# Another order of the loads and of GpSimd's operations in an RWKV-7 recurrence with a wave mixer

## The chip, the cores and the metric

The kernel runs on one core of a Trainium2 chip. The metric is device microseconds of one execution. Times of several executions are given as a median with the lowest and highest; the profile is of one more execution, whose span (first to last instruction) is a little shorter than its time.

## The reference

Two stages, one after the other. The first is a recurrence over 768 tokens for 4 x 8 heads with 40 features:

```python
for t in range(S):
    y[:, :, t] = np.einsum('bhd,bhde->bhe', rt, state)
    Sa = np.einsum('bhde,bhe->bhd', state, at)
    state_decay = state * wt[:, :, None, :] - np.einsum('bhd,bhe->bhde', Sa, bt)
    state = state_decay + np.einsum('bhd,bhe->bhde', vt, kt)
```

The second takes y as x, of 4 x 768 x 320, and mixes tokens and channels:

```python
theta = x @ w_theta
zr, zi = x * np.cos(theta), x * np.sin(theta)
u = x + einsum('ts,bsd->btd', w_tok_r, zr) + einsum('ts,bsd->btd', w_tok_i, zi)
out = u + np.maximum(u @ w_ch, 0.0)
```

## The kernel before, in words

The tokens are cut into 24 chunks of 128, six for each of the four batches. A chunk's six inputs (w, k, b, a, v, r) are loaded from HBM in the arrangement of the recurrence, so w, k, b and a come as 1024 pieces of 160 bytes (`load`, line 409); r, and v of the first eight chunks, come two chunks at a time in longer pieces (`loads`, line 421). For a chunk ScalarE takes the logarithm of w (L445), TensorE sums it over the tokens, ScalarE takes exponentials (L469, L479, L487). GpSimd scales k, b and a with them (`product`, L429; the tiles kb and ah) and casts v and r (`cast`, L435). TensorE transposes these (L391, L538), makes four score matrices (L569), which VectorE or ScalarE masks on the way out of PSUM (L578, L580; where ScalarE does it, GpSimd clears the other triangle, L582), and forms the state and the output x (L610 to L684, L793 to L802). VectorE adds the state's old value to the new (the tile sum, L663) and GpSimd scales it (gt, L667).

The mixer follows in pieces. Pairs of chunks of x are transposed (L711) and multiplied by w_theta (L763, L773). Once a batch has its six chunks, or half of them, ScalarE computes sine and cosine (cs, L850, with a change of its function table before and after, the table loads at L850 and L1024), GpSimd multiplies by x (zr and zi, L865), and TensorE mixes the tokens (L881, twelve matmuls of a 128-token block with zr and zi of all six chunks). The token weights come in 12 loads of 128 rows that GpSimd's queue issues (`wtok_block`, L960, tiles wrow_r and wrow_i), which convert to bf16 on the way; TensorE transposes them (L968). The two other weights are loaded by GpSimd's queue as well (`mixer_weights`, L932).

The program is a list of some 1600 operations, each with its engine. They are made in the order of the algorithm and issued in the order of the written-out list `ORDER` (line 26); `PICK` says which operations run on their second engine, `HOMES` which PSUM bank each result gets. Each engine runs its instructions strictly in that order and waits for semaphores of the others. SyncE issues the 180 loads, stores and transposing DMAs in the list's order as well. Besides waiting for its buffer to be free, each DMA of SyncE waits for the one eight places before it in its queue, so up to eight are under way.

Filler matmuls (`WARM`, L1019) are put ahead of a few of TensorE's operations at the start.

Of the kernel before, what the change touches and what calls it, by code (L numbers as in the profile page):

```python
# [26 lines left out]
    0, 7, 3, 6, 1, 2, 20, 8, 21, 23, 24, 4, 27, 9, 32, 30, 5, 22, 31, 33, 12, 25, 26, 34, 11,  # L27
    28, 10, 69, 35, 36, 29, 70, 37, 18, 47, 44, 40, 19, 48, 72, 45, 38, 41, 71, 49, 73, 39, 46,
    98, 119, 76, 99, 58, 14, 42, 100, 74, 57, 15, 13, 120, 122, 101, 50, 121, 79, 75, 51, 123,
    53, 106, 102, 107, 131, 108, 80, 52, 16, 77, 109, 132, 125, 78, 43, 103, 81, 17, 110, 134,  # L30
    126, 111, 133, 82, 56, 84, 137, 54, 104, 124, 138, 112, 129, 83, 85, 87, 130, 88, 127, 55,
    156, 86, 128, 59, 157, 89, 146, 184, 143, 90, 147, 105, 158, 61, 97, 60, 139, 187, 159,
    135, 62, 144, 148, 164, 96, 188, 160, 165, 191, 140, 93, 136, 145, 161, 166, 141, 91, 185,
    167, 213, 186, 92, 194, 214, 149, 189, 142, 162, 168, 150, 215, 163, 169, 190, 216, 195,
    152, 221, 170, 234, 151, 246, 192, 222, 235, 193, 237, 217, 95, 236, 202, 238, 218, 94,
    196, 203, 197, 63, 241, 155, 247, 171, 267, 248, 219, 239, 199, 198, 172, 220, 223, 205,
    249, 200, 240, 271, 64, 244, 272, 242, 299, 245, 201, 154, 273, 224, 243, 300, 173, 301,
    261, 206, 254, 274, 302, 225, 174, 262, 303, 279, 153, 175, 258, 306, 176, 255, 212, 259,
    263, 280, 250, 177, 204, 281, 256, 211, 275, 496, 282, 260, 320, 226, 251, 305, 257, 208,
    252, 276, 264, 283, 253, 317, 207, 227, 349, 327, 265, 277, 497, 328, 304, 309, 278, 329,  # L40
    498, 284, 266, 310, 270, 499, 330, 350, 285, 307, 351, 268, 318, 286, 354, 308, 269, 331,
    352, 500, 311, 361, 332, 319, 287, 314, 353, 312, 209, 336, 333, 539, 362, 210, 337, 289,
    356, 288, 315, 363, 313, 322, 290, 364, 338, 355, 291, 387, 325, 292, 339, 316, 365, 540,
    388, 359, 366, 389, 541, 357, 360, 340, 390, 341, 382, 358, 391, 321, 116, 503, 113, 501,
    542, 412, 373, 181, 342, 334, 376, 374, 502, 392, 367, 411, 326, 504, 377, 375, 506, 335,
    393, 368, 505, 323, 178, 369, 545, 524, 394, 378, 370, 507, 517, 525, 413, 508, 372, 526,
    384, 371, 509, 395, 416, 396, 527, 532, 417, 528, 397, 510, 511, 514, 529, 544, 117, 595,
    512, 572, 533, 415, 383, 530, 118, 398, 573, 515, 596, 513, 554, 385, 399, 534, 531, 574,
    418, 597, 401, 535, 400, 516, 575, 414, 402, 543, 379, 324, 404, 114, 567, 598, 536, 403,
    546, 548, 115, 380, 581, 642, 576, 582, 555, 601, 549, 577, 381, 583, 599, 66, 386, 550,  # L50
    584, 537, 557, 568, 600, 551, 182, 522, 558, 602, 183, 585, 586, 538, 619, 578, 561, 587,
    419, 179, 518, 559, 547, 604, 519, 556, 427, 180, 428, 421, 429, 605, 560, 420, 606, 520,
    423, 552, 607, 626, 553, 562, 434, 422, 627, 564, 435, 425, 436, 565, 563, 643, 628, 424,
    437, 644, 610, 566, 629, 426, 613, 645, 603, 588, 611, 630, 231, 523, 571, 521, 589, 438,
    430, 570, 698, 635, 631, 646, 612, 439, 431, 636, 632, 440, 608, 745, 432, 614, 699, 647,
    609, 746, 700, 675, 648, 747, 637, 433, 615, 676, 616, 701, 293, 569, 633, 677, 748, 634,
    651, 649, 638, 678, 590, 652, 684, 296, 579, 685, 679, 617, 639, 228, 620, 621, 580, 653,
    706, 657, 591, 654, 680, 592, 618, 686, 650, 593, 661, 703, 687, 594, 441, 622, 711, 702,
    640, 442, 681, 712, 662, 688, 655, 658, 705, 656, 689, 659, 641, 663, 660, 682, 704, 664,
    690, 749, 667, 683, 665, 691, 68, 709, 692, 707, 67, 710, 729, 668, 65, 670, 672, 666, 708,  # L60
    694, 693, 750, 624, 695, 730, 719, 713, 697, 751, 720, 731, 696, 232, 732, 294, 233, 297,
    714, 721, 295, 733, 738, 298, 229, 734, 739, 715, 716, 230, 740, 735, 717, 754, 450, 752,
    451, 778, 755, 718, 346, 625, 452, 779, 453, 741, 343, 623, 756, 881, 780, 454, 757, 408,
    882, 781, 742, 405, 673, 671, 764, 883, 767, 765, 669, 782, 884, 444, 722, 455, 783, 443,
    768, 456, 766, 445, 784, 446, 736, 457, 885, 785, 458, 760, 737, 743, 447, 459, 753, 448,
    786, 787, 887, 744, 761, 796, 788, 769, 758, 460, 759, 789, 763, 461, 888, 762, 790, 462,
    797, 912, 463, 792, 791, 913, 793, 723, 770, 795, 892, 771, 914, 794, 674, 893, 915, 886,
    772, 802, 890, 464, 891, 803, 773, 347, 465, 916, 348, 344, 799, 917, 905, 805, 409, 345,
    406, 726, 920, 407, 804, 896, 811, 466, 921, 473, 897, 725, 410, 474, 808, 475, 918, 724,
    467, 809, 468, 898, 922, 469, 899, 798, 927, 476, 449, 471, 477, 919, 906, 900, 801, 889,  # L70
    928, 470, 478, 929, 960, 728, 807, 480, 901, 930, 481, 961, 955, 923, 482, 806, 962, 483,
    963, 894, 935, 727, 484, 931, 479, 924, 800, 969, 895, 485, 908, 970, 940, 486, 983, 932,
    964, 941, 902, 965, 1030, 971, 907, 934, 903, 925, 972, 1031, 776, 819, 933, 820, 1032,
    926, 487, 904, 810, 821, 1033, 488, 822, 775, 984, 936, 966, 985, 774, 938, 986, 823, 1035,
    937, 824, 939, 777, 489, 1086, 973, 825, 490, 987, 1007, 491, 1034, 949, 494, 946, 942,
    812, 492, 813, 950, 1087, 957, 1037, 814, 1088, 974, 1036, 943, 1089, 951, 815, 975, 956,
    945, 816, 990, 944, 817, 947, 958, 1041, 1039, 989, 1042, 976, 909, 818, 1040, 988, 948,
    1014, 911, 977, 826, 1015, 991, 952, 910, 1052, 827, 953, 1016, 1090, 967, 1058, 994, 1017,
    992, 968, 959, 1053, 954, 995, 979, 993, 978, 1008, 1018, 1133, 1054, 996, 1019, 980, 998,
    997, 1001, 981, 1020, 1009, 999, 828, 982, 1023, 1002, 1092, 1134, 1010, 829, 1024, 1000,  # L80
    830, 1091, 1135, 1004, 1110, 1049, 1005, 1136, 835, 1093, 1011, 836, 833, 1095, 831, 1003,
    1063, 1012, 1050, 1096, 837, 838, 1064, 1097, 1006, 1038, 1021, 1065, 1098, 1022, 1051,
    1013, 1025, 1066, 1104, 1045, 1026, 1043, 1072, 1061, 1044, 839, 1105, 840, 1060, 1073,
    1067, 1027, 1046, 1059, 1068, 1266, 1074, 841, 1047, 1069, 1267, 1161, 1075, 1048, 1028,
    1094, 1268, 1117, 1111, 1138, 1099, 1029, 1118, 1076, 1055, 1101, 1269, 1100, 1139, 1119,
    1137, 1056, 1077, 1112, 1120, 1140, 1070, 1126, 1071, 1142, 1102, 1057, 1106, 1127, 1062,
    1144, 1143, 1121, 1113, 1128, 1312, 1103, 1122, 1107, 1145, 1078, 865, 1123, 1108, 1115,
    866, 1129, 867, 1313, 1141, 1166, 1290, 1148, 1314, 1124, 1114, 1130, 1155, 1167, 1315,
    1152, 1125, 1156, 1270, 1146, 1291, 1168, 1273, 1149, 1169, 868, 1153, 1157, 1147, 869,
    1272, 1150, 1131, 1116, 1151, 1271, 1079, 1154, 1132, 1162, 870, 1080, 1170, 1109, 871,  # L90
    1277, 1316, 1292, 1275, 1171, 1278, 1340, 1158, 1367, 1276, 1317, 1172, 1159, 1297, 1173,
    1081, 1318, 1163, 1368, 1082, 1298, 1083, 1274, 1164, 1369, 1281, 1174, 1284, 1319, 1342,
    1084, 1370, 1299, 1085, 1321, 1282, 1293, 1300, 1320, 842, 1327, 843, 844, 1322, 1283,
    1165, 1301, 1305, 845, 1302, 846, 1185, 1285, 1323, 1345, 1341, 1306, 847, 1187, 1160,
    1324, 1343, 1307, 1346, 1286, 1184, 1331, 848, 1347, 1175, 1332, 1295, 1348, 1186, 858,
    1349, 859, 1344, 1373, 1176, 1333, 860, 1308, 861, 1325, 1191, 1407, 1354, 862, 1326, 1355,
    863, 1372, 1350, 1309, 1408, 1371, 1310, 864, 1409, 1351, 849, 1467, 1311, 1334, 1356, 850,
    1190, 1410, 1294, 1279, 1335, 1177, 1280, 1412, 1391, 1178, 1328, 1296, 1392, 1374, 1357,
    851, 1336, 1330, 852, 1329, 853, 1375, 1411, 1393, 1352, 854, 1358, 1394, 1287, 1414, 856,
    1353, 1303, 1400, 1288, 1304, 1179, 1413, 1401, 1395, 1468, 1180, 1469, 1188, 1396, 1289,  # L100
# [956 lines left out]
```

## Time and profile before

| | |
|---|---|
| median of 3 runs | 198.48 us (198.17 to 200.91) |
| the profiled execution | 199.53 us, its span 197.8 us |
| granted TensorE clock | 1.0 over the whole span |
| busy: PE, DVE, ACT, POOL | 187.6, 164.3, 151.7, 145.1 us |
| DMA | 32.75 MB in 134644 packets, 124816 of them under 512 bytes |
| queue of SyncE's loads (q1), queue of GpSimd's (q0) | 75.1% and 9.6% of 16 engines' span |

An engine's idle time before an instruction stands in brackets in the timelines, with what ended it. PE is TensorE; its matmuls are pipelined, and their ends are modelled. SPq, ACTq and POOLq are the sequencers that issue DMAs.

### The profile page before, as it was taken

To read this page: it belongs to the slowest core of one execution; us is meant where nothing else is said; L and a number is where in the kernel's file an instruction comes from. 1 tells how busy PE (TensorE), PEld (TensorE's weight loads), DVE (VectorE), ACT (ScalarE), POOL (GpSimd) and SP (SyncE) were. 2 spreads that over 40 slices of the span, in tenths; PEclk is the share of its full clock that TensorE was granted. 3 is DMA by queue.
4 is the path that set the end of the run, shared out by engine and by line. 5 is a ranking of instruction groups with operands and counts; after the bars stand their busy time and mean duration, and the time that the engine had idled before them with its cause. 6 is when DMAs were issued, how large, how long until landed. Compare 5 with 4: busy or idle time off the path is not lost.

```text
span 197.8 us, 8019 instructions
## 1 busy us (share of the span) xinstructions
PE 187.6 (95%) x3288; PEld 150.3 (76%) x3288; DVE 164.3 (83%) x261; ACT 151.7 (77%) x337; POOL 145.1 (73%) x210
## 2 busy tenths in 40 slices
PE   7888999999989999999999999999999999999992
PEld 6776787777768788878878888888887878767661
DVE  5269899999989999888887988999999988675453
ACT  3584979799889988979988598888998986575111
POOL 8267544679879999699799939769699697558100
PEclk9999999999999999999999999999999999999999
DMA  6999879989999999999998899988998274863055
GB/s 119 210 212 163 154 161 196 182 166 197 233 174 173 207 171 185 190 185 223 153 210 168 153 187 170 188 148 169 182 155 163 43 177 102 87 194 104 0 191 174
DMA packets 134644, 32.75 MB, mean 166 GB/s; under 512 B 124816, under 2 KB 134608, under 8 KB 134608
## 3 DMA queue, kind: packets, MB, share of 16 engines
q1 hardware_dynamic: 131680, 29.19, 75.1%
q0 software_dynamic: 2784, 2.97, 9.6%
q8 instruction: 25, 0.41, 0.9%
q10 hardware_dynamic: 144, 0.08, 0.1%
q14 instruction: 11, 0.09, 0.1%
HBM read 29.54 MB, written 3.93 MB: 169 GB/s over the span
## 4 chain that ended last, share of the span: by engine, by line
PE 68%; DMA 9%; ACT 8%; SPq 6%; DVE 3%; issue 3%; POOL 1%; ACTq 0%; DVEq 0%; POOLq 0%
PE ps_s L881 17%; PE ps_s L391 10%; PE ps_d L569 9%; PE ps_s L763 5%; SPq L409 4%; DMA raw_w<-in_w_dram 3%; DMA raw_kb<-in_k_dram 3%; PE ps_s L711 3%; PE ps_s L652 2%; PE ps_s L629 2%; SPq L421 2%; DMA raw_r<-in_r_dram 2%; PE ps_s L538 2%; PE ps_s L773 2%; ACT cs L850 2%
## 5 line engine op out<-in xcount | busy, mean ns | idle before, releaser
L429 POOL TENSOR_TENSOR kb<-raw_kb,ex 128x320 bf16<-128x320 f32 x46 | 36.8, 811 | 9.7 <-DMA raw_kb<-in_k_dram 3.3
L881 PE MATMUL ps_s<-zr,wtok_r 128*128 128x320 bf16 x132 | 37.6, 299 | 0.0
L881 PE MATMUL ps_s<-zi,wtok_i 128*128 128x320 bf16 x132 | 37.5, 299 | 0.0
L578 DVE TENSOR_TENSOR lamu<-ps_d,mask_p 128x1024 bf16<-128x1024 f32 x22 | 26.8, 1219 | 1.7 <-PE ps_d L569 1.6
L578 DVE TENSOR_TENSOR psi<-ps_d,mask_p 128x1024 bf16<-128x1024 f32 x22 | 26.8, 1218 | 1.6 <-PE ps_d L569 1.4
L578 DVE TENSOR_TENSOR lamv<-ps_d,mask_p 128x1024 bf16<-128x1024 f32 x17 | 20.7, 1218 | 2.6 <-PE ps_d L569 1.8
L429 POOL TENSOR_TENSOR ah<-raw_a,we 128x320 bf16<-128x320 f32 x22 | 19.0, 866 | 3.6 <-DMA raw_a<-in_a_dram 1.6
L578 DVE TENSOR_TENSOR phi<-ps_d,mask_n 128x1024 bf16<-128x1024 f32 x17 | 20.7, 1218 | 0.9 <-PE ps_d L569 0.8
L865 POOL TENSOR_TENSOR zi<-cs,xp 128x320 bf16<-128x320 f32 x21 | 16.9, 816 | 3.3 <-ACT cs L850 3.3
L881 PEld LDWEIGHTS <-wtok_r 128*128 128x128 bf16 x144 | 14.0, 97 | 4.5
L569 PE MATMUL ps_d<-aT,kbT 64*128 64x128 bf16 x384 | 17.1, 217 | 0.2
L881 PEld LDWEIGHTS <-wtok_i 128*128 128x128 bf16 x144 | 14.1, 98 | 3.5
L391 PE MATMUL ps_s<-wide,kb 128*128 128x128 bf16 x184 | 15.0, 223 | 1.0 <-POOL kb L429 0.7
L865 POOL TENSOR_TENSOR zr<-cs,xp 128x320 bf16<-128x320 f32 x19 | 15.3, 810 | 0.7 <-ACT cs L850 0.7
L667 POOL TENSOR_TENSOR gt<-sum,ex 128x320 bf16<-128x320 f32 x13 | 9.5, 733 | 8.0 <-DVE sum L663 4.8
L800 PE MATMUL ps_s<-kb,lamv 128*128 128x40 bf16 x192 | 15.0, 180 | 0.0
L802 PE MATMUL ps_s<-kb,lamu 128*128 128x40 bf16 x192 | 14.9, 179 | 0.0
L569 PEld LDWEIGHTS <-kbT 64*128 64x128 bf16 x384 | 11.8, 94 | 3.1 <-ACT kbT L394 1.0
L800 PEld LDWEIGHTS <-lamv 128*128 128x128 bf16 x192 | 13.2, 96 | 0.6
L887 DVE TENSOR_TENSOR up<-ps_s,xp 128x320 bf16<-128x320 f32 x22 | 10.7, 488 | 3.5 <-PE ps_s L881 3.1
L435 POOL CAST r<-raw_r 128x640 bf16<-128x640 f32 x12 | 8.6, 720 | 6.5 <-DMA raw_r<-in_r_dram 6.5
L445 ACT ACTIVATE lw<-raw_w 128x320 bf16<-128x320 f32 x24 | 11.4, 475 | 2.6 <-DMA raw_w<-in_w_dram 2.6
(176 smaller groups left out, 606.7 us busy)
## 6 DMA issues: line engine op xcount, KB each, us to landing
raw_w<-in_w_dram SPq DMA_DIRECT2D x24, 160.0 KB, 4.1
raw_v<-in_v_dram SPq DMA_DIRECT2D x24, 160.0 KB, 3.9
raw_a<-in_a_dram SPq DMA_DIRECT2D x24, 160.0 KB, 4.2
raw_kb<-in_k_dram SPq DMA_DIRECT2D x24, 160.0 KB, 3.7
raw_kb<-in_b_dram SPq DMA_DIRECT2D x24, 160.0 KB, 4.0
raw_r<-in_r_dram SPq DMA_DIRECT2D x24, 160.0 KB, 4.4
out_dram<-oo SPq DMA_DIRECT2D x9, 160.0 KB, 2.0
wrow_i<-in_moe_w_tok_i_dram POOLq DMA_DIRECT2D x6, 192.0 KB, 5.3
```

The costliest lines, as they stand in the source:

```text
L391: nc.tensor.transpose(out=dst[:, c:c + 128], in_=pair(src, g), identity=ident)
L429: pool = ("POOL", lambda: nc.gpsimd.tensor_tensor(out=dst, in0=in0, in1=in1, op=ALU.mult))
L445: add("ACT", "ln", i, lambda: nc.scalar.activation(out=paired(lw)[:, :, :, 0:D], in_=paired(raw_w[s4]), func=AF.Ln), 473, [("raw_w", s4)], ...
L569: nc.tensor.matmul(t[:, q, g, :], lhsT=lhs[g][rows(q)], rhs=rhs[g][rows(q)], start=True, stop=True)
L578: add("DVE", kindm, i, lambda: nc.vector.tensor_tensor(out=flat, in0=whole(), in1=mask.to_broadcast([128, 2 * G, 128]), op=ALU.mult), 1217 ...
L667: add("POOL", "wgt", i, lambda: nc.gpsimd.tensor_tensor(out=new_state, in0=sum_t, in1=wm.to_broadcast([128, 8, D]), op=ALU.mult), 830, [(" ...
L763: nc.tensor.matmul(ps(pk)[:, 0:DM], lhsT=lhs[:, 3 * c + kt, :], rhs=wt[:, 3 * c + kt, :], start=kt == 0, stop=kt == 2, skip_group_check=n ...
L800: nc.tensor.matmul(o, lhsT=lamv[:, p, g, :], rhs=kb[:, 0, h, 0:D], start=first, stop=False, skip_group_check=True)
L802: nc.tensor.matmul(o, lhsT=lamu[:, p, g, :], rhs=kb[:, 1, h, 0:D], start=False, stop=True, skip_group_check=True)
L865: pool = ("POOL", lambda: nc.gpsimd.tensor_tensor(out=dst, in0=in0, in1=in1, op=ALU.mult))
L881: nc.tensor.matmul(acc(), lhsT=wtok[nm][j][:, s], rhs=zs[c][:, s], start=n == 0 and c == 0, stop=n == NT - 1 and c == 1)
L887: add("DVE", "uadd", q, lambda: nc.vector.tensor_tensor(out=u, in0=acc(), in1=x, op=ALU.add), 488, [pk, x_key(q)], [u_key(q)], at="row")
```

## The change

Only the list `ORDER` differs: the same operations in another order. PE's, DVE's and ACT's own sequences come out the same; SyncE's and GpSimd's do not. The diff replaces the whole list; its first lines and those with the later token loads (operations 181 and 178):

```diff
-    0, 7, 3, 6, 1, 2, 20, 8, 21, 23, 24, 4, 27, 9, 32, 30, 5, 22, 31, 33, 12, 25, 26, 34, 11,
+    0, 3, 7, 6, 1, 20, 2, 21, 23, 8, 24, 27, 4, 30, 32, 31, 22, 33, 5, 25, 12, 34, 11, 26, 69,
...
-    542, 412, 373, 181, 342, 334, 376, 374, 502, 392, 367, 411, 326, 504, 377, 375, 506, 335,
-    393, 368, 505, 323, 178, 369, 545, 524, 394, 378, 370, 507, 517, 525, 413, 508, 372, 526,
...
+    396, 527, 384, 181, 418, 413, 532, 528, 397, 510, 178, 511, 529, 514, 545, 417, 595, 117,
```

In words, with positions counted in each engine's own sequence from 0 (a letter with a number is a load or an operation of that chunk; z(c, j) is the product zr or zi of chunk j of a batch):

SyncE, 180 positions. Moved are:
- 1 to 11: a0 ahead of half of v0; r0's second half, w2 and a1 one earlier, k1 from 8 to 11.
- 35 to 38: b5 ahead of w6, k5 ahead of k6.
- 50 to 55: w9 and k8 one earlier, r8's first half from 50 to 52; w10 and a8 change places.
- 60 to 70: w11 behind v9, w12, k10, b10, a10 and v11 two or three earlier; k11 from 62 to 70, r10's first half from 63 to 67.
- 77 to 97: b13 from 77 to 80, k14 from 85 to 87, v14 from 89 to 86, others by one.
- 128 to 145: v20, r20, b21, v21 earlier by two to five, w22, k22, b22, b23 later by three to five, others by one to three.

GpSimd, 185 positions, of which 18 are issues of weight loads. Moved are:
- 13 and 14 (k and b of chunk 3); 20 to 22 and 24, 25: the cleared lamv of chunk 3, b5, v6's cast one earlier, a5's product two later.
- 29 to 59: the first two token loads come directly one after the other (29 and 31 become 29 and 30), k7 and b7 one earlier, a7 two later. The third and fourth token load go from 33 and 35 to 36 and 39, behind r6's cast (36 becomes 35). Batch 0's first products: one goes from 45 to 34, one from 44 to 37, one from 39 to 45, the others move by one or two; k8 and b8 come one and three later. Token load wrow_i of block 4 goes from 59 to 53, ahead of batch 0's second six products.
- 60 to 91: neighbours change places; token loads of blocks 5 and 6 one and two earlier, w_ch's second load two earlier, phi of chunk 12 two earlier and psi of chunk 12 four later.
- 92 to 107: batch 1's products in another order, with v14's cast from 102 to 95, k14 and b14 three and four earlier.
- 108 to 154: mostly neighbours; batch 2's first products move by up to eight, lamv of chunk 17 four later, of chunk 18 three earlier, b21 two earlier, b22's k two later.
- From 155 on nothing moves.

185 rows, old and new, of the table ORDER are left out of this document.

## The prediction

> **What bounds it now.** I read the page first, then busy time by stretches, then the chain of waits where TensorE is not full, then the timelines of the queues that the change reorders.
>
> ```profile
> PE 187.6 (95%) x3288; PEld 150.3 (76%) x3288; DVE 164.3 (83%) x261; ACT 151.7 (77%) x337; POOL 145.1 (73%) x210
> ...
> PE 68%; DMA 9%; ACT 8%; SPq 6%; DVE 3%; issue 3%; POOL 1%; ACTq 0%; DVEq 0%; POOLq 0%
> ```
>
> ```profile
> 0.00:40.00 40.00, 35.75 (x628) 29.27 (x629) 30.57 (x61) 28.04 (x69) 23.89 (x49) 1.00 0.90 176
> 40.00:60.00 20.00, 18.38 (x371) 14.86 (x367) 18.86 (x24) 18.26 (x44) 16.83 (x24) 1.00 1.02 190
> 60.00:160.00 100.00, 99.46 (x1871) 81.80 (x1870) 91.53 (x134) 88.71 (x195) 87.23 (x121) 1.00 0.94 171
> 160.00:198.00 38.00, 34.03 (x431) 24.39 (x428) 23.32 (x44) 16.68 (x32) 17.13 (x20) 1.00 0.50 127
> ```
>
> The columns are the stretch, its length, then PE, PEld, DVE, ACT, POOL. TensorE carries 68% of the chain and is the bound. Its idle time is length minus busy: 40.00 - 35.75 = 4.25 us before 40 us, 1.62 us from 40 to 60, 0.54 us in the hundred after that, 3.97 us in the tail. A change that leaves TensorE's list alone can win only idle time, and the tail's operations are not touched. So the gain has to come from before 60 us, and a loss can come from anywhere that a GpSimd product or a load becomes late.
>
> The loads are the trouble before 60 us: DMA share 0.90 and 1.02. One of them stands in the chain. This is the chain of waits from 44 to 60 us, then ScalarE's, VectorE's and TensorE's timelines around that place.
>
> ```profile
> 48.11 6.82 DMA raw_w<-in_w_dram
> ...
> 54.95 0.03 ACT lw L445
> ...
> 55.33 0.36 ACT nuT L394
> ```
>
> ```profile
> 52.66 1.28 ACT L1024 ACT_TABLE_LOAD   x1
> 54.95 0.47 ACT L445 ACTIVATE lw<-raw_w 128x320 bf16<-128x320 f32 x1 [1.01 <-DMA raw_w<-in_w_dram]
> ```
>
> ```profile
> 56.88 1.23 DVE L578 TENSOR_TENSOR lamu<-ps_d,mask_p 128x1024 bf16<-128x1024 f32 x1 [0.60 <-PE ps_d L569]
> ```
>
> ```profile
> 54.58 0.30 PE L679 MATMUL ps_s<-wide,gt 128*128 128x80 bf16 x4
> 55.73 0.44 PE L711 MATMUL ps_s<-wide,xp 128*128 128x128 bf16 x5 [0.85 <-ACT nuT L394]
> ```
>
> The load of w for chunk 9 is issued at 48.11 and lands 6.82 us later. ScalarE, done with its table load at 52.66 + 1.28 = 53.94, waits for it until 54.95. Behind that logarithm is queued the copy of nuT, and for the bank that this copy frees TensorE's transposes at L711 wait 0.85 us. This is the largest single stall after 10 us.
>
> **The change part by part.** The lists of PE, DVE and ACT are the same instruction for instruction; only SyncE's and GpSimd's move.
>
> ```profile
> 45.01 0.60 POOL L960 DMA_DIRECT2D wrow_i<-in_moe_w_tok_i_dram  x1
> ...
> 46.43 0.59 POOL L960 DMA_DIRECT2D wrow_r<-in_moe_w_tok_r_dram  x1
> ...
> 47.80 0.59 POOL L960 DMA_DIRECT2D wrow_i<-in_moe_w_tok_i_dram  x1
> ...
> 49.18 0.59 POOL L960 DMA_DIRECT2D wrow_r<-in_moe_w_tok_r_dram  x1
> 50.15 0.71 POOL L435 CAST r<-raw_r 128x640 bf16<-128x640 f32 x1 [0.38 <-DMA raw_r<-in_r_dram]
> ...
> 55.64 0.80 POOL L429 TENSOR_TENSOR kb<-raw_kb,ex 128x320 bf16<-128x320 f32 x1 [1.66 <-DMA raw_kb<-in_k_dram]
> ```
>
> ```profile
> 45.81 0.54 SPq L409 DMA_DIRECT2D raw_kb<-in_b_dram  x1
> 46.44 1.57 SPq L421 DMA_DIRECT2D raw_r<-in_r_dram  x1
> 48.11 0.55 SPq L409 DMA_DIRECT2D raw_w<-in_w_dram  x1
> 48.70 1.37 SPq L409 DMA_DIRECT2D raw_kb<-in_k_dram  x1
> ```
>
> ```profile
> q0 software_dynamic: 573, 0.78, 58.9%
> ```
>
> Loads at 46 to 49 us. Chunk 9's w and chunk 8's k go ahead of the half of r (46.44). So w is issued at 46.44 instead of 48.11. Even if it still takes 6.82 us it lands at 53.26, before ScalarE asks at 53.94. And it should take less: the four token-weight loads hold 58.9% of the DMA engines from 46 to 54 us (q0, last row), 0.589 x 8 / 4 = 1.18 us of all 16 engines each, and two of them are moved behind. The stall of 1.01 us goes. What is late next: nuT then ends near 54.67, TensorE has its matmuls of L679 out of the way by 54.88, so L711 starts near 54.8 in place of 55.73: 0.9 us. VectorE's lamu moves up by its 0.60 us of idle time at once and more behind it. GpSimd must give the same: its wait of 1.66 us is for chunk 8's k, which now is issued at 48.1 instead of 48.70 and has less traffic beside it; with products in the gap before it GpSimd reaches this kb by hand count (0.60, 0.75 to 0.82 and 0.86 us an instruction from 45.0 on, r held to 50.15) at 55.0. It is then about a microsecond ahead as well. I take 0.9 us, between 0 (if it is lost again) and 1.0 (the wait itself).
>
> Two token loads later. They are issued at about 50.8 and 52.9 instead of 47.80 and 49.18, on GpSimd's queue behind r and one and three products.
>
> ```profile
> DMA to landing us min/median/max: 5.2/5.4/5.6
> ```
>
> ```profile
> 62.70 0.51 PE L968 MATMUL ps_s<-wide,wrow_r 128*128 128x128 bf16 x6
> ```
>
> At the longest landing time of this tile, 5.6 us, the second lands at 58.5; the later of its two readers starts at 62.70. Cost zero; if the cover of 4 us were used up, TensorE would wait in its own list. The 2 x 1.18 us of transfers now lie beside the loads of chunk 9, which wait for GpSimd, not GpSimd for them.
>
> First loads (positions 1 to 11). Half of r is one seat earlier and chunk 1's k three later.
>
> ```profile
> 11.34 0.78 PE L1019 MATMUL ps_s<-busy 128*128 128x128 bf16 x11
> 11.95 0.61 PE L538 MATMUL ps_s<-wide,r 128*128 128x128 bf16 x8
> ```
>
> The reader of r stands behind eleven filler matmuls until 11.95, so an earlier r wins nothing; the load of b that holds chunk 1 keeps its seat. Zero. Loads 35 to 38 (b and k of chunk 5 ahead of w and k of chunk 6): TensorE is not idle before their readers, zero.
>
> The other moves of GpSimd, 62 to 160 us: I laid its new list over the trace with the durations above, each operation at the later of its inputs and its predecessor. With one exception no reader that TensorE has is brought nearer than 0.2 us, and TensorE has 0.54 us of idle time there in all. Zero, from -0.3 to the price of the exception, which is the rival below. Loads after chunk 19 move up to five seats with 3 us or more to spare by the same count: zero.
>
> Sum: 0.9 us off the profiled execution. Its span is 197.8 us and its time 199.53 us, 1.05 us above the median of 198.48; so 198.6 for that execution and 198.48 - 0.9 = 197.6 us as a median.
>
> **The rivals.** No change after all: the lead of 0.9 us at 56 us is spent before the end, as VectorE, ScalarE and GpSimd have only 8 to 13 us of room in the hundred microseconds that follow and one late product takes it. For it: the tightness. Against it: nothing in those rows is tied to a clock other than the loads. 198.5 us.
>
> The token load collides earlier. The second of the four (46.43) moves up to about 45.4, since its neighbours change places, and so competes for a microsecond more with the half of r that GpSimd awaits at 50.15. If each side gets half of the engines, r is 0.5 us later, and TensorE, which already waits 0.35 us for it, passes that on to ScalarE's table load: the gain shrinks to 0.4 us, 198.1 us. The Trainium skill, page "DMA: Bandwidth & Descriptors", section "Queues, rings and completion order", says that each DMA engine takes turns between the queue rows that have work, one packet at a time; by that rule alone the sum would be 0.4 and not 0.9. The trace neither proves nor excludes it: q0 took 58.9% and the loads 52.0% of the same 8 us.
>
> Slower: GpSimd blocked at the cast of v for chunk 14. It moves ahead of seven products; three stand between it and chunk 13's kb, as many as run now up to 94.78 + 1.54 = 96.3 us, where GpSimd then reaches it.
>
> ```profile
> 94.78 1.54 POOL L865 TENSOR_TENSOR zi<-cs,xp 128x320 bf16<-128x320 f32 x2
> 97.39 0.80 POOL L865 TENSOR_TENSOR zi<-cs,xp 128x320 bf16<-128x320 f32 x1 [1.07 <-ACT cs L850]
> ...
> 102.86 0.44 POOL L435 CAST v<-raw_v 128x320 bf16<-128x320 f32 x1
> ...
> 106.38 0.79 POOL L865 TENSOR_TENSOR zr<-cs,xp 128x320 bf16<-128x320 f32 x1
> ```
>
> ```profile
> 108.32 0.30 PE L881 MATMUL ps_s<-zr,wtok_r 128*128 128x320 bf16 x1
> ```
>
> ```profile
> L409 SPq DMA_DIRECT2D raw_v<-in_v_dram x1: 722/722/722, 95.6 to 95.6; - x1
> ...
> DMA to landing us min/median/max: 3.7/3.7/3.7
> ```
>
> Its load lands now at 95.6 + 3.7 = 99.3. If it still did, GpSimd would sit 3.0 us instead of the 1.07 it sits now, and the last zr, which has 108.32 - 107.17 = 1.15 us to spare, would be 0.8 late: TensorE waits, and as a load's landing is tied to the clock the lead is lost as well: 198.48 + 0.8 = 199.3. It decides from a landing at about 98.5. Against it: the load moves up three seats, to
>
> ```profile
> L409 SPq DMA_DIRECT2D raw_v<-in_v_dram x1: 2519/2519/2519, 90.1 to 90.1; - x1
> ...
> DMA to landing us min/median/max: 6.3/6.3/6.3
> ```
>
> the seat that starts at 90.1 and lands at 96.4, which costs GpSimd nothing beyond what it idles today.
>
> More gain: r lands earlier too, with less traffic behind it, and all 1.62 us of TensorE's idle time from 40 to 60 us goes: 196.9 us.
>
> **How the numbers follow.** Forecast 0.47, with a range of its own of 197.2 to 198.0; no change 0.20; the collision 0.10; blocked at v 0.13; more gain 0.10. The range must reach both ends of the last two without their outer halves: 196.8 to 199.3. All the cases lie within 2% of 198.48 (3.97 us, about what a measurement of this kernel can tell from no change); beyond it I leave 0.02 for faster and 0.03 for slower, in which several readers are late at once, and 0.95 for the same.
>
> **What would show it.** Right: ScalarE's L445 at the place of 54.95 has no wait for raw_w, L711 behind it none of 0.85, and GpSimd's kb none of 1.66; TensorE's idle time from 40 to 60 us is 0.8 us rather than 1.6, and 60 to 160 stays below 1. Wrong: a wait of TensorE on GpSimd's r of over 0.8 us at 50 us (the collision); an idle GpSimd of over 2 us before a cast of v near 97 us, and L881 waiting on zr (the blocked cast); or no wait at 54 us and yet the old span, with new idle time of TensorE after 60 us.

## The result, and the profile after

The changed kernel takes 199.35 us in the median of 22 runs (198.03 to 202.24); the kernel before takes 198.50 us beside it (22 runs, 197.74 to 200.91). The ratio is 1.0057 (95% interval 1.0035 to 1.0078); it leaves out the few executions more than 1.5% above the fastest of their kernel, so it is not the quotient of the two medians. The forecast was 197.6 us: by the ratio the change loses 1.1 us (by the medians 0.85 us) where a gain of 0.9 us was expected. Its profiled execution took 200.56 us, with a span of 198.8 us.

These are the engines' line and the chain's line of its page, then the busy time by stretches: the columns are again the stretch, its length, PE, PEld, DVE, ACT, POOL, the granted clock, the DMA share and GB/s.

```profile
PE 187.1 (94%) x3288; PEld 150.0 (75%) x3288; DVE 163.7 (82%) x261; ACT 151.6 (76%) x337; POOL 145.5 (73%) x210
...
PE 60%; DMA 9%; SPq 8%; POOL 8%; ACT 8%; issue 4%; DVE 1%; POOLq 0%; ACTq 0%; DVEq 0%
```

```profile
0.00:40.00 40.00, 35.66 (x641) 29.34 (x642) 30.71 (x63) 28.45 (x70) 24.26 (x50) 0.96 0.91 180
40.00:60.00 20.00, 18.13 (x368) 14.93 (x367) 19.26 (x24) 18.43 (x45) 16.88 (x24) 1.00 0.99 178
60.00:160.00 100.00, 98.29 (x1843) 80.37 (x1840) 89.33 (x132) 86.87 (x190) 86.08 (x118) 1.00 0.94 170
160.00:198.00 38.00, 35.05 (x448) 25.36 (x446) 24.46 (x45) 17.82 (x34) 18.27 (x21) 1.00 0.51 130
```

TensorE's share of the chain has fallen from 68% to 60% and GpSimd's has risen from 1% to 8%. Between 60 and 160 us TensorE now idles 1.71 us instead of 0.54, and from 40 to 60 us 1.87 us where 0.8 was announced.

The promised gain is there all the same. ScalarE's and TensorE's timelines at the place of the old stall:

```profile
51.47 1.28 ACT L1024 ACT_TABLE_LOAD   x1
52.77 0.47 ACT L445 ACTIVATE lw<-raw_w 128x320 bf16<-128x320 f32 x1
53.15 0.35 ACT L394 COPY nuT<-ps_s 128x256 f32<-128x256 f32 x1
```

```profile
53.39 0.30 PE L679 MATMUL ps_s<-wide,gt 128*128 128x80 bf16 x4
53.55 0.44 PE L711 MATMUL ps_s<-wide,xp 128*128 128x128 bf16 x5
```

No bracket stands behind L445 or L711: both waits are gone, and L711 starts at 53.55 us instead of 55.73. Here is where the lead goes, on GpSimd, then on TensorE, and in ScalarE's timeline at 57 us:

```profile
53.43 0.80 POOL L429 TENSOR_TENSOR kb<-raw_kb,ex 128x320 bf16<-128x320 f32 x1
56.63 0.72 POOL L435 CAST r<-raw_r 128x640 bf16<-128x640 f32 x1 [2.40 <-DMA raw_r<-in_r_dram]
...
58.80 0.86 POOL L429 TENSOR_TENSOR ah<-raw_a,we 128x320 bf16<-128x320 f32 x1
...
74.75 0.45 POOL L435 CAST v<-raw_v 128x320 bf16<-128x320 f32 x1 [0.96 <-DMA raw_v<-in_v_dram]
75.98 0.80 POOL L429 TENSOR_TENSOR kb<-raw_kb,ex 128x320 bf16<-128x320 f32 x1 [0.78 <-DMA raw_kb<-in_k_dram]
76.74 0.71 POOL L435 CAST r<-raw_r 128x640 bf16<-128x640 f32 x1
```

```profile
58.44 0.41 PE L569 MATMUL ps_d<-rT,nuT 64*128 64x128 bf16 x8 [0.42 <-ACT nuT L394]
59.72 0.40 PE L391 MATMUL ps_s<-wide,ah 128*128 128x128 bf16 x4 [0.88 <-POOL ah L429]
...
77.50 0.62 PE L538 MATMUL ps_s<-wide,r 128*128 128x128 bf16 x8 [0.92 <-POOL r L435]
...
80.53 0.40 PE L391 MATMUL ps_s<-wide,kb 128*128 128x128 bf16 x4 [0.31 <-POOL kb L429]
```

```profile
57.65 0.47 ACT L445 ACTIVATE lw<-raw_w 128x320 bf16<-128x320 f32 x1 [0.72 <-DMA raw_w<-in_w_dram]
```

The old stall is back one chunk later, only smaller: ScalarE waits 0.72 us for w of chunk 10, the copy of nuT is queued behind that logarithm as before, and TensorE waits 0.42 us for it at 58.44. (In the second profile of the changed kernel these two waits are 0.71 and 0.55 us.)

GpSimd's old wait of 1.66 us (for k of chunk 8) has become one of 2.40 us for the second half of r of chunk 8; the product a of chunk 8 is queued behind it, and TensorE waits 0.88 us for that one. Twenty microseconds on, GpSimd's casts of v and r of chunk 10 and its kb of chunk 11 make TensorE wait again, 0.92 and 0.31 us. The chain has two loads that take long, the second half of r of chunk 8 and then b of chunk 11:

```profile
50.51 5.97 DMA raw_r<-in_r_dram
...
72.18 7.43 DMA raw_kb<-in_b_dram
```

Followed from operation to operation, TensorE's start in the changed kernel against the kernel before is 1.19 us earlier at 51 us, 2.18 earlier at L711 (the main term: 0.99 us), 0.61 earlier at the transposes of a of chunk 8, 0.89 later at r of chunk 10, 1.41 later at 79 us and 1.02 later at the end. (The lead of 1.19 us at 51 us is not evidence for the change: a kernel with the old order up to 60 us, middle_alone below, is 1.20 us earlier there.) Nothing is gained or lost beyond 0.4 us after 80 us. The question is what happens between 56 and 80 us.

### The profile page after: what moved, and what is told of

Its sections match the earlier page's. It is cut to its first block, busy times and chain, and to the rows that moved or that the text cites. A ratio compares the mean times of both kernels' runs of the same rounds, so it can differ in the third digit from the quotient of the medians.

```text
span 198.8 us, 8015 instructions
## 1 busy us (share of the span) xinstructions
PE 187.1 (94%) x3288; PEld 150.0 (75%) x3288; DVE 163.7 (82%) x261; ACT 151.6 (76%) x337; POOL 145.5 (73%) x210
## 4 chain that ended last, share of the span: by engine, by line
PE 60%; DMA 9%; SPq 8%; POOL 8%; ACT 8%; issue 4%; DVE 1%; POOLq 0%; ACTq 0%; DVEq 0%
PE ps_s L881 15%; PE ps_s L391 9%; PE ps_d L569 8%; PE ps_s L763 5%; SPq L409 5%; DMA raw_kb<-in_b_dram 4%; SPq L421 3%; DMA raw_r<-in_r_dram 3%; DMA raw_a<-in_a_dram 3%; PE ps_s L629 2%; PE ps_s L711 2%; PE ps_s L773 2%; PE ps_s L652 2%; PE ps_s L538 2%; ACT cs L850 2%
## 5 line engine op out<-in xcount | busy, mean ns | idle before, releaser
L445 ACT ACTIVATE lw<-raw_w 128x320 bf16<-128x320 f32 x24 | 11.4, 475 | 2.9 <-DMA raw_w<-in_w_dram 2.9
L469 ACT ACTIVATE ex<-ps_s 128x328 f32<-128x328 f32 (+1 forms) x24 | 10.6, 447 | 3.5 <-PE ps_s L458 1.4
```

Of the source, the lines that this page charges most:

```text
L445: add("ACT", "ln", i, lambda: nc.scalar.activation(out=paired(lw)[:, :, :, 0:D], in_=paired(raw_w[s4]), func=AF.Ln), 473, [("raw_w", s4)], ...
L469: got = add("ACT", "exp", i, lambda: nc.scalar.activation(out=ex[:, :, 0:D] if no_total else ex.rearrange("p h x -> p (h x)"), in_=sums(ps ...
```

## The experiments

In the diffs a line is a stretch of one engine's own sequence of `ORDER` (SP for SyncE, POOL for GpSimd); the positions count from 0. All the other engines are always as they were. Every kernel was measured beside the kernel before on the same chip.

**One engine's order at a time.** The first two kernels have the whole of one engine's new sequence; the next two have the new order of both in one stretch of time only.

```diff
 sync_alone: SP 0-179 as in the change, POOL as before
 gpsimd_alone: SP as before, POOL 0-184 as in the change
 front_alone:
-SP 50-55: 325, 382, 321, 326, 323, 517
+SP 50-55: 382, 321, 325, 326, 517, 323
-POOL 30-45: 503, 113, 501, 181, 502, 178, 369, 545, 413, 416, 417, 544, 415, 554, 418, 414
+POOL 30-45: 113, 501, 503, 502, 414, 369, 181, 418, 413, 178, 545, 417, 544, 554, 415, 416
-POOL 47-48: 601, 66
+POOL 47-48: 66, 601
 middle_alone:
-SP 60-70: 567, 386, 568, 522, 619, 518, 519, 520, 523, 571, 521
+SP 60-70: 386, 567, 619, 518, 519, 520, 571, 522, 523, 521, 568
...
-POOL 67-69: 657, 650, 703
+POOL 67-69: 650, 703, 657
```

Expected of the loads alone:

> The kernel before, with the loads in their new order and GpSimd's list as it was (its token loads too). Theory A, the loss is made by the loads from chunk 10 on: in the changed kernel the load of k of chunk 11 is eight places later and the load of b of chunk 11 lands at 79.60 us instead of 74.77, so that GpSimd's kb of chunk 11 starts at 79.67 instead of 77.82. With the loads alone that stays, so this one is slower: 199.3 us (198.9 to 199.8). Rival B, the loss is made by GpSimd's own order (the cast of r of chunk 10 two operations later, which TensorE's transposes waited for at 77.5 us): then only the main term of the prediction is left here, 197.9 us (197.5 to 198.3). Rival C, the loss comes after 85 us, from the order of block 8's and 11's products: also 197.9 us.

Expected of GpSimd's list alone:

> The kernel before, with GpSimd's list in its new order (the token loads later) and the loads as they were. Theory A (the loads from chunk 10 on make the loss): the loss is away, and most of the gain at 55 us too, since w of chunk 9 still lands at 54.9 us: 198.4 us (198.0 to 198.8). Rival B (GpSimd's order makes it): 199.4 us (199.0 to 199.9). Rival C (block 8's and 11's products after 85 us): 199.4 us, with TensorE no later than before at 80 us and later at 100 us.

Expected of the stretch of 45 to 60 us alone:

> The kernel before, with only the stretch of 45 to 60 us changed: w of chunk 9 and k of chunk 8 ahead of r of chunk 8, w of chunk 10 ahead of a of chunk 8, the two token loads of block 3 and six products of block 2 in their new places. The trace of the changed kernel has TensorE 2.2 us earlier at the transposes of x at 53.6 us and only 0.6 us earlier at the transposes of a of chunk 8 at 59.7 us, for GpSimd waited 2.4 us there for r of chunk 8, whose load lands at 56.5 us in both. Theory A: what is left of the lead, 0.6 us, goes through to the end, and nothing takes it: 197.9 us (197.5 to 198.2). Rival D: the lead is lost at the next loads in any order, since the queue of loads is the bound there (75% of its time busy): 198.5 us (198.3 to 198.7).

Expected of the stretch of 60 to 85 us alone:

> The kernel before, with only the stretch of 60 to 85 us changed: the loads from k of chunk 11 to v of chunk 10, and GpSimd's list from the cast a of chunk 9 to the weights of chunk 10. Theory A: here is the whole loss, TensorE is 1.4 to 1.6 us later at 81 us than in this kernel without it: 199.8 us (199.3 to 200.2). Rival C (the loss is made after 85 us): 198.5 us (198.2 to 198.7). Rival D (the queue of loads is the bound, and the order inside it does not matter): 198.5 us.

Measured: the loads alone 198.48 us, ratio 0.9973 (0.9937 to 1.0008); GpSimd's list alone 200.85 us, 1.0108 (1.0073 to 1.0144); the front alone 0.9985 (0.9951 to 1.0018); the middle alone 0.9998 (0.9966 to 1.0031). Theory A falls: the new loads do no harm by themselves, and GpSimd's list costs a full per cent by itself. B had the direction of both; of the second it expected 0.9 us, and 2.1 us came. The middle alone rules out A's 199.8 us; the front alone fits both of its values, 197.9 and 198.5 us. What GpSimd's list does on the old loads is seen in GpSimd's timeline and then in TensorE's:

```profile
69.62 0.80 POOL L429 TENSOR_TENSOR kb<-raw_kb,ex 128x320 bf16<-128x320 f32 x1 [1.87 <-DMA raw_kb<-in_b_dram]
70.38 0.73 POOL L667 TENSOR_TENSOR gt<-sum,ex 128x320 bf16<-128x320 f32 x1
```

```profile
71.16 0.20 PE L610 MATMUL ps_s<-gt,aT 128*128 128x80 bf16 x1 [1.80 <-POOL gt L667]
```

The new list puts kb of chunk 10 ahead of gt of chunk 8; kb waits for its load, gt with it, and TensorE behind gt. It is a place that the changed kernel, whose load of b of chunk 10 is two seats earlier, doesn't show.

**GpSimd's list by parts, and the kernel before once more.** On the new loads, GpSimd's new order only up to 60 us, only from 60 to 85 us, only after 85 us.

```diff
 SP 0-179 as in the change, and
 loads_gp_front: POOL 0-49 as in the change, 50-184 as before
 loads_gp_middle: POOL 50-80 as in the change, the rest as before
 loads_gp_late: POOL 81-184 as in the change, the rest as before
 before_again: no change to the kernel before
```

> All loads in the new order, and of GpSimd's list only the first part new (up to 60 us: the token loads of block 3 later, six products of block 2 earlier, r of chunk 8 ahead of two of them). With the new loads and GpSimd's old list the ratio to the kernel before was 0.9973 (0.9937 to 1.0008), with the new list and the old loads 1.0108, with both 1.0057. Theory E1, GpSimd's loss lies here: in the changed kernel it stood 2.40 us before the cast of r of chunk 8 and TensorE's lead fell from 2.18 to 0.61 us: 199.4 us (199.0 to 199.9). Theory E2, the loss lies between 60 and 85 us: 198.0 us (197.6 to 198.4). Theory E3, it lies after 85 us: 198.0 us.

> All loads in the new order, and of GpSimd's list only the stretch of 60 to 85 us new (the load of wrow_i of block 4 six operations earlier, kb of chunk 10 ahead of gt of chunk 8, r of chunk 10 behind kb of chunk 11). Theory E2, GpSimd's loss lies here: with the new list and the old loads TensorE fell from 1.43 us ahead to 0.50 us behind between 64 and 71 us, since kb of chunk 10 stood ahead of gt of chunk 8 on GpSimd and waited for a load that took 6.01 us beside the token load; and in the changed kernel it lost 2.0 us between 60 and 80 us: 199.4 us (199.0 to 199.9). Theories E1 (before 60 us) and E3 (after 85 us): 198.0 us (197.6 to 198.4).

> All loads in the new order, and of GpSimd's list only what comes after 85 us new (the products of blocks 8 and 11, the casts of v and kb of chunk 14, and on to the end). Theories E1 and E2: 198.0 us (197.6 to 198.4), for in every trace so far TensorE runs from 100 us to the end like in the kernel before, only shifted as a whole (1.41 us at 81 us and 1.02 us at the end in the changed kernel). Theory E3, the loss lies here: 199.4 us (199.0 to 199.9).

> The kernel before itself, once more, for a second profiled execution of it. Theory N, the wait of ScalarE for w of chunk 9 at 54.95 us (1.01 us) and TensorE's 0.85 us behind it, which the prediction's main term removes, belong to that one execution (199.53 us, against a median of 198.5 over its runs): with the same orders up to 60 us, the kernel that changes only the stretch of 60 to 85 us had TensorE 2.07 us earlier at 56.8 us without the change of loads. Then this execution has no such wait, TensorE's transposes of x of block 4 start at 53.5 to 54.5 us, and the time is 198 to 199 us. Theory M, the wait belongs to the order: it is here again, with 0.7 us or more of idle time of TensorE behind nuT, and the transposes start at 55.2 us or later.

Measured: front 200.37 us, 1.0105 (1.0054 to 1.0157); middle 199.17 us, 1.0020 (0.9983 to 1.0057); late 198.58 us, 0.9990 (0.9953 to 1.0027). E1 fits best: the one loss clear of the scatter sits in GpSimd's first part (a repeat below is smaller), and the part after 85 us, where the prediction had its slower rival, shows no cost.

The kernel before against itself gave 1.0046 (1.0006 to 1.0087). That is the measure for every single ratio here: executions of one kernel differ by about a microsecond, and half a per cent in one comparison is no difference. Its second profile has the stall again, in ScalarE's timeline and in TensorE's:

```profile
55.10 0.47 ACT L445 ACTIVATE lw<-raw_w 128x320 bf16<-128x320 f32 x1 [1.03 <-DMA raw_w<-in_w_dram]
```

```profile
55.88 0.44 PE L711 MATMUL ps_s<-wide,xp 128*128 128x128 bf16 x5 [0.87 <-ACT nuT L394]
```

So the stall belongs to the old order (theory M), though not to every execution of it. The kernel with only the middle changed has the old order up to 60 us, and there L445 and L711 ran at 52.88 and 53.66 us without a wait. Two of three executions with the old order have it.

**The two token loads.** GpSimd's first part holds the two loads of block 3 (operations 181 and 178), which the prediction put at zero. They were moved alone, both ways.

```diff
 tokens_back: the changed kernel, with
-POOL 30-39: 113, 501, 503, 502, 414, 369, 181, 418, 413, 178
+POOL 30-39: 113, 501, 503, 181, 502, 178, 414, 369, 418, 413
 front_tokens_back: loads_gp_front with the same edit
 loads_tokens_later: sync_alone with
-POOL 30-39: 503, 113, 501, 181, 502, 178, 369, 545, 413, 416
+POOL 30-39: 503, 113, 501, 502, 369, 545, 181, 413, 416, 178
 tokens_later: the kernel before with the same edit
```

> The changed kernel, with only the two token loads of block 3 (wrow_i, wrow_r, 192 KB each) put back to their old seats on GpSimd, three and four operations earlier. With new loads and the first part of GpSimd's new list the ratio was 1.0105 (1.0054 to 1.0157), with new loads and the other parts 1.002 and 0.999, so the loss sits in GpSimd's first part; that part holds the two token loads and casts and products. Theory T, the token loads: issued at 49.2 and 51.3 us instead of 46.8 and 48.2 they run beside r, a of chunk 8 and w of chunk 10, which land 1 to 3 us later (a of chunk 8 at 58.43 in the changed kernel, at 56.38 with the new loads alone): 198.3 us here (197.9 to 198.8). Rival F, the order of the casts and products before 50 us: no better than the changed kernel, 199.4 us (199.0 to 199.9). A kernel measured against itself gave 1.0046 in these runs, so half a per cent alone is not read as a difference.

> All loads in the new order, GpSimd's old list, and in it only the two token loads of block 3 three and four operations later. Theory T: the token loads make the whole loss of GpSimd's first part, 200.0 us (199.4 to 200.6), against 198.5 with the new loads alone. Rival F (the casts and products of the first part make it): 198.2 us (197.7 to 198.7).

> All loads in the new order, the first part of GpSimd's list (up to 60 us) new, but the two token loads of block 3 in their old seats. Theory T: 198.2 us (197.7 to 198.7), 1% under the 1.0105 of the same kernel with the token loads later. Rival F: 200.0 us (199.4 to 200.6).

> The kernel before, with only the two token loads of block 3 three and four operations later: the part of the change that the prediction put at zero, by itself. In the old order w of chunk 9 and k of chunk 8 run beside them and land 6.8 us after their issue. Theory T1, a token load that comes later frees w of chunk 9 and hurts the loads behind it as much: 198.5 us (198.1 to 198.9). Theory T2, it hurts more than it frees also here, since the loads behind (a of chunk 8, w of chunk 10, b of chunk 9) are what the next 10 us wait for: 199.5 us (199.1 to 200.0). Rival F: 198.2 us, the wait for w of chunk 9 is shorter and nothing else changes.

Measured: the changed kernel with them back 199.07 us, 1.0019 (0.9986 to 1.0052); the new loads with them later 199.20 us, 0.9988 (0.9949 to 1.0028), its executions from 196.92 to 202.24; GpSimd's new first part with them back 198.16 us, 0.9960 (0.9933 to 0.9987), against 1.0105 with them later; the kernel before with them later 198.16 us, 0.9993 (0.9962 to 1.0023). Theory T holds for the front. For the kernel before T2 falls; T1 and F lie too close to be told apart by the time, though in the trace TensorE gains 0.99 us at L711 and gives back 0.6 us by 60 us, as T1 has it. The changed kernel comes out between T and F, and with GpSimd's old casts around them the seats made no measurable difference in time: the new loads with them later miss theory T's 200.0 us.

**Does it repeat, and through which load?** The pair of the front was measured again, both on one chip, with two kernels in which b of chunk 11, the 7.43 us load of the chain, is issued three seats earlier.

```diff
 front_b11: loads_gp_front, and after_b11: the changed kernel, each with
-SP 67-72: 522, 523, 521, 568, 570, 569
+SP 67-72: 522, 523, 569, 521, 568, 570
...
 front_again: loads_gp_front; tokens_back_again: front_tokens_back
```

> All loads in the new order and GpSimd's first part new with the late token loads (ratio 1.0105 so far), and one load moved: b of chunk 11 three seats earlier on SyncE, ahead of v of chunk 10, k and a of chunk 11. Its buffer has been free since 47 us. Theory P, the late token loads cost the time at this load: in the three profiles with new loads and late token loads it was issued at 70.9 to 72.2 us, among three token loads of blocks 4 and 5, took 6.5 to 7.6 us and TensorE lost 0.5 to 1.8 us at 79 us; three seats earlier (2 us) it lands by 75 us: 199.0 us (198.5 to 199.6), with GpSimd's second kb of chunk 11 without its wait. Theory Q, they cost it at a and r of chunk 8 at 56 to 60 us: no better, 200.3 us (199.7 to 200.9).

> The changed kernel with the same one load, b of chunk 11, three seats earlier. Theory P: 198.7 us (198.2 to 199.2), TensorE loses nothing between 77 and 81 us. Theory Q: 199.4 us (199.0 to 199.9), the changed kernel's own time.

> The same kernel as the one with the ratio 1.0105 (new loads, GpSimd's first part new, token loads late), a second time, beside the next. If that ratio was no chance of one chip: 200.3 us (199.7 to 200.9), a ratio of 1.006 to 1.014. If it was: 199.0 us, 1.000 to 1.004.

> The same kernel as the one with the ratio 0.996 (new loads, GpSimd's first part new, the two token loads of block 3 in their old seats), a second time. Theory T (the seats of the token loads decide): 198.0 us (197.5 to 198.5), a ratio of 0.993 to 0.999, over a per cent under the kernel with late token loads. If the first result was chance: 198.8 us, 0.999 to 1.003.

Measured: front_again 199.26 us, 1.0029 (0.9989 to 1.0069), tokens_back_again 197.86 us, 0.9976 (0.9944 to 1.0007). The first 1.0105 did not repeat in size; the direction did. Set against each other (here and below from the logarithms of the executions that the ratios use), the late seats take 1.0053 times as long (1.0013 to 1.0092). The load of b of chunk 11 is not the one place: front_b11 gave 1.0010 (0.9971 to 1.0049) and after_b11 1.0103 (1.0053 to 1.0153), worse than the changed kernel. For the changed kernel theory P falls, and Q, which expected no change, doesn't explain the worse result either; in the front the difference (1.0010 against 1.0029) is within the intervals and settles nothing. GpSimd's timeline in after_b11, then TensorE's, show what happened instead:

```profile
74.78 0.45 POOL L435 CAST v<-raw_v 128x320 bf16<-128x320 f32 x1 [2.30 <-DMA raw_v<-in_v_dram]
```

```profile
76.91 0.62 PE L538 MATMUL ps_s<-wide,r 128*128 128x128 bf16 x8 [1.23 <-POOL r L435]
```

A load that made room, v of chunk 10, became the late one: GpSimd waits 2.30 us for it instead of 0.96, and r is cast behind it.

**The changed kernel itself, both ways on one chip.**

```diff
 after_again: the changed kernel; tokens_back_third: tokens_back
```

> The changed kernel itself, a second time. It gave 1.0057 (1.0035 to 1.0078). Theory T, the late token loads cost it its gain: 199.5 us, a ratio of 1.003 to 1.009, and in the profile TensorE loses more than 0.5 us between 56 and 95 us against the kernel before. Rival N, the ratio is the scatter of executions between chips: 1.000 or less, no loss between 56 and 95 us.

> The changed kernel with only the two token loads of block 3 back in their old seats, a second time. Theory T: 198.4 us, a ratio of 0.996 to 1.002, at least 0.4% under the changed kernel beside it, and in the profile no loss over 0.3 us between 56 and 95 us. Rival N: the same as the changed kernel beside it.

Measured, on a chip on which the kernel before took 200.96 us: the changed kernel 203.08 us, 1.0142 (1.0082 to 1.0202); with the two token loads back 200.81 us, 1.0040 (0.9996 to 1.0084). Against each other 1.0094 (1.0046 to 1.0142), so theory T holds in its main point for the change as a whole. Its details were off: the changed kernel lies above the expected 1.003 to 1.009, and with the token loads back TensorE still loses 1.0 us between 56 and 95 us where 0.3 at most was expected. That rest points to GpSimd's other moves: tokens_back and front_tokens_back, which differ only in GpSimd's list from 60 us on, were on one chip, and the first takes 1.0043 times as long (1.0007 to 1.0078). This is no more than the kernel before once differed from itself, so it is not shown to be a cost in time.

**All profiles side by side.** TensorE's idle time (length less busy) in two stretches of each profiled execution, with the ratio. These are the rows of five of them: the kernel before, the changed kernel twice, then the two with its token loads back.

```profile
56.00:100.00 44.00, 43.91 (x827) 36.00 (x824) 39.38 (x56) 40.92 (x91) 40.68 (x58) 1.00 1.06 183
```

```profile
10.00:56.00 46.00, 43.59 (x886) 35.48 (x881) 41.90 (x53) 39.16 (x98) 32.26 (x42) 0.99 0.98 185
56.00:100.00 44.00, 41.27 (x762) 33.58 (x762) 37.15 (x54) 37.61 (x82) 39.41 (x55) 1.00 1.01 176
```

```profile
56.00:100.00 44.00, 41.15 (x765) 32.74 (x763) 37.20 (x51) 37.54 (x86) 38.39 (x54) 1.00 1.03 180
```

```profile
56.00:100.00 44.00, 43.74 (x816) 35.95 (x813) 39.85 (x58) 40.41 (x88) 40.46 (x58) 1.00 1.03 183
```

```profile
56.00:100.00 44.00, 43.22 (x823) 35.57 (x820) 39.33 (x55) 39.57 (x90) 39.44 (x55) 1.00 1.01 177
```

| kernel | token loads of block 3 | idle 10-56 us | idle 56-100 us | ratio |
|---|---|---|---|---|
| before, before_again | old | 3.77, 4.44 | 0.09, 0.09 | 1, 1.0046 |
| sync_alone, loads_gp_late | old | 2.20, 2.51 | 0.21, 0.21 | 0.9973, 0.9990 |
| front_tokens_back, tokens_back_again | old | 3.04, 3.96 | 0.21, 0.09 | 0.9960, 0.9976 |
| tokens_back, tokens_back_third | old | 2.67, 4.27 | 0.26, 0.78 | 1.0019, 1.0040 |
| middle_alone, loads_gp_middle | old | 2.20, 2.43 | 1.21, 1.59 | 0.9998, 1.0020 |
| tokens_later, front_alone | late | 1.96, 3.00 | 0.74, 1.61 | 0.9993, 0.9985 |
| loads_tokens_later | late | 1.73 | 3.01 | 0.9988 |
| loads_gp_front, front_again | late | 2.49, 2.30 | 2.87, 1.45 | 1.0105, 1.0029 |
| gpsimd_alone | late | 2.61 | 2.65 | 1.0108 |
| after, after_again | late | 2.41, 3.27 | 2.73, 2.85 | 1.0057, 1.0142 |
| after_b11 | late | 1.67 | 3.24 | 1.0103 |

(front_b11 is left out: its profiled execution took 203.71 us, 4 us over its median.) With the token loads late TensorE idles 0.74 to 3.24 us between 56 and 100 us, 2.65 or more in six of nine; with them in their old seats 0.09 to 0.26 in seven of ten, and 0.78 to 1.59 in three. Late token loads are not the only way to lose time there: in middle_alone and loads_gp_middle about 1 us of it (1.05 and 0.98) is TensorE's wait at 59 us for a of chunk 8, with GpSimd held up before by k of chunk 8 (2.08 and 1.58 us), and up to there both have GpSimd's old list. In tokens_back_third 0.56 us is the wait for r of chunk 10, cast behind k of chunk 11. From 100 to 160 us it is 0.16 to 0.46 us in all of them.

**Which loads pay.** From issue to landing, in us, in the changed kernel and in tokens_back, with only the two token loads back (one execution of each; w9 is w of chunk 9, and so on):

| | w9 | k8 | r8, second half | w10 | a8 | b9 |
|---|---|---|---|---|---|---|
| token loads late | 6.2 | 6.1 | 6.0 | 6.4 | 6.6 | 6.0 |
| in their old seats | 7.5 | 8.7 | 4.5 | 4.5 | 4.7 | 3.6 |

The shares of the DMA engines by queue fit this. From 51 to 58 us of the changed kernel, and then from 50.5 to 57 us of the other, most of the time in which r8, w10, a8 and b9 are under way (packets, MB, share; q0 has the token loads):

```profile
q1 hardware_dynamic: 3265, 0.80, 57.9%
q0 software_dynamic: 277, 0.38, 31.4%
```

```profile
q1 hardware_dynamic: 5245, 1.11, 84.1%
q0 software_dynamic: 113, 0.14, 12.2%
```

The same token traffic lies beside other loads. This agrees with the Trainium skill, page "DMA: Bandwidth & Descriptors", section "Queues, rings and completion order", by which each DMA engine goes round the queue rows that have work, packet by packet. That what GpSimd's queue sends lengthens SyncE's loads beside it is our reading of the table, not a sentence of that page. With the loads back, GpSimd waits 1.02 us for k8 and 0.26 us for r8:

```profile
53.79 0.81 POOL L429 TENSOR_TENSOR kb<-raw_kb,ex 128x320 bf16<-128x320 f32 x1 [1.02 <-DMA raw_kb<-in_k_dram]
54.86 0.72 POOL L435 CAST r<-raw_r 128x640 bf16<-128x640 f32 x1 [0.26 <-DMA raw_r<-in_r_dram]
```

and reaches a of chunk 8 at 57.05 us instead of 58.80. When the late seats are dear is open. They cost time with all the new loads and GpSimd's new first part. With GpSimd's old casts they showed no cost in time (loads_tokens_later, tokens_later), and neither did they with its new casts and only the loads of 45 to 60 us in the new order (front_alone, 0.9985). One profile of each kernel is too little to tell why.

## Why the prediction was wrong

**The stall at 54.95 us: right in the trace, not seen in full in the time.** From the transposes of r before it to L711, TensorE gains 0.99 us in the changed kernel, 1.00 in its second profile and 1.00 with the loads alone; 0.9 was said. But it was two cures for one stall. The kernel before with only the token loads later, w9 in its old seat, gains 0.99 us there as well. In the profiles the wait at L445 is gone in all ten with the token loads late; with the new loads and the token loads in their old seats it is gone in five of seven and 0.36 and 0.27 us in the other two. So the sum had to count the gain once and the second cure's price in full. And the 0.9 us were taken off the median in full, though they were read from one execution, 1.05 us above that median, and one of three executions with the old order has no such stall. The loads alone gain 0.27% (0.9937 to 1.0008), about 0.5 us, and that is not clear of zero.

**The two token loads: the step that failed.** "Cost zero", the prediction said, looking at their own readers, who indeed never waited in any of the ten profiles with the late seats; and of their transfers, that they "now lie beside the loads of chunk 9, which wait for GpSimd, not GpSimd for them". They lie beside r and a of chunk 8, w of chunk 10 and b of chunk 9. GpSimd does wait for one of them (2.40 us for r), with a product behind that TensorE waits for (0.88 us), and ScalarE waits for another (0.72 us for w of chunk 10), with TensorE behind it (0.42 us). In GpSimd's new list the price is 0.5% to 0.9% of the time, 1.0 to 1.9 us by the two pairs that were each on one chip, instead of zero; that is as much as the whole forecast gain or more. One pair alone would hardly stand out from the 0.46% by which the kernel before differed from itself; the two agree in direction, and the second is twice that. In the old list the same move had no measurable price (0.9993), so it is a price of this place in this order, not of the move by itself.

**GpSimd's other moves: the waits were missed, their price is open.** The count over the trace held the landings of the loads where they were. In the changed kernel the cast of v of chunk 10 and the product of k of chunk 11 stand ahead of the cast of r of chunk 10. They wait 0.96 and 0.78 us for their loads, the second of which the change had issued eight seats later, and TensorE then waits 0.92 us for r. In the pair on one chip GpSimd's moves after 60 us take 0.43% (0.07% to 0.78%), 0.9 us, which by itself is no more than the scatter. With the old loads those moves are not free: GpSimd's whole list costs 1.08% there and its token loads alone nothing measurable (0.9993, on another chip). The rival that GpSimd is blocked at a cast of v was the right kind of event at the wrong chunk: the part of the list with chunk 14 shows no cost.

**First loads and loads 35 to 38, loads after chunk 19:** nothing speaks against zero, but none was tried by itself. The loads alone are 0.9973 (0.9937 to 1.0008), and from 108 us on TensorE's shift against the kernel before moves by 0.4 us or less in every profile.

**The collision with r of chunk 6** (the rival at 198.1 us) is not in the changed kernel's first profile, where that cast runs at 48.52 us without a wait. It does occur in other kernels with the new first part of GpSimd's list: GpSimd waits 0.89 us for that r in gpsimd_alone and 0.84 in loads_gp_front, and TensorE behind it 0.87 and 0.61 us. With the token loads back on the last chip TensorE waited too, but GpSimd itself waited for the load only 0.28 us there, so that wait is not shown to be the collision.

```profile
51.95 0.62 PE L538 MATMUL ps_s<-wide,r 128*128 128x128 bf16 x8 [1.10 <-POOL r L435]
```

**The signs named.** The last sign of a wrong forecast is the one that came: no wait at 54 us, and yet the old span or more, with new idle time of TensorE after 60 us. Against the rival "no change after all" the prediction had said that nothing is tied to a clock other than the loads. The loads were tie enough: GpSimd's three longest waits between 50 and 85 us in the changed kernel (2.40, 0.96 and 0.78 us) are all for loads.

A version that keeps the cure of the seat and leaves out the late token loads, front_tokens_back, was measured twice: 0.9960 (0.9933 to 0.9987) and 0.9976 (0.9944 to 1.0007), 198.16 and 197.86 us. It is ahead of the changed kernel. It is also about 0.3% ahead of the kernel before, which is less than that one once differed from itself. It stands 0.3 to 0.6 us above the forecast.

## What to carry to other kernels

When a stretch is full of transfers, moving a transfer out of one load's way puts it into another's: find who is under way at the new place and who waits for those, not only who reads the moved one. Ask also whether the next load of the same kind now has the same stall. If two edits cure the same stall, count the gain once and price the second edit by itself. And lay a new order of an in-order engine over landings that move with it: an operation placed ahead of another hands on every wait for its own load.

## What the runs showed of the hardware that was not expected

Executions of one kernel on one core, at a granted clock of 0.99 to 1.0, spread over 3 us (197.35 to 200.36 us for the kernel before, beside the first four experiments). In the traces two executions of one kernel part before 108 us: the two of loads_gp_front still run level at 79 us (1.47 and 1.31 us ahead of the kernel before) and are 2.2 us apart at 108. From there to the end TensorE's shift against the kernel before changes by 0.4 us or less in the profiles, whatever it is by then (from 2.3 us earlier to 4.0 us later). Six loads of 160 KB took from 3.6 to 8.7 us from issue to landing in two executions whose kernels differ in the seats of two other transfers.
